# Linear attention on one core: the sum over a head's partitions for rows 0 to 511, made by four transfers inside SBUF and two adds on VectorE instead of one matrix product

## The chip, the core and the metric

The kernel runs on one core of a Trainium2 chip. The core has five engines that work side by side, each through its own list of instructions in order: TensorE (PE in the profile, with its weight loads listed as PEld), VectorE (DVE), ScalarE (ACT), GpSimd (POOL) and SyncE (SP), which here issues the transfers (DMA). Engines wait for each other through semaphores. SBUF is the on-chip memory of 128 partitions; PSUM, of eight banks of 128 x 512 f32, takes the results of matrix products.

The metric is the device time of one execution in microseconds (us), the median of several runs.

## What is computed

The reference, cut to what matters, with B = 1, S = 2048 rows, D = 640, H = 32 heads of Dh = 20:

```python
qkv = (x @ wqkv).reshape(B, S, 3, H, Dh)          # then split into q, k, v by heads
phi = lambda t: where(t > 0, t + 1, exp(t)) + 1e-6
pq, pk = phi(q), phi(k)
kv  = einsum("bhsd,bhse->bhde", pk, v)            # 20 x 20 per head
z   = einsum("bhsd->bhd", pk)                     # sum of pk over all rows
num = einsum("bhqd,bhde->bhqe", pq, kv)
den = einsum("bhqd,bhd->bhq", pq, z) + 1e-6       # one number per row and head
o   = num / den
out = o.reshape(B, S, D) @ wo
```

The change is about `den`: for every row and head the sum of 20 products of `pq` and `z`.

## The kernel before

**Layout.** The columns of q are reordered so that `pq` lies in SBUF as five chunks c = 0..4 of 128 partitions by 2048 rows of the sequence. A head's 20 columns are then 4 neighbouring partitions in each of the 5 chunks: head h has partitions 4h to 4h+3. The sequence is worked on in four blocks s = 0..3 of 512 rows.

**Stages.** First comes k: `k_half` (L292) for 16 row tiles, with `k_phi` making `pk` from it. Then `p_step` (L319) accumulates x^T pk over the 16 row tiles in five PSUM banks, first for the left half of the columns (h = 0) and then for the right half (h = 1); in the code one call of `p_step(h, st)` is one row tile, five products of 320 columns. Between these steps, at places written out by hand in the loops at the end of the kernel, stand *q tiles*: `next_q` calls `q_tile` (L345), five products of 512 columns into one bank, then an exponential on ACT (L353), then a min (L357) and a multiply-and-add (L360) on DVE, which leave one chunk of one block of `pq`. There are 20 q tiles, block by block.

After the right half, `p_out` copies the five banks to `pt` (ACT L331 for chunks 0, 2, 4; DVE L334 for chunks 1 and 3), `kv_group` (L423) multiplies that with the v weights, `kv_mask` (L440) keeps the diagonal blocks, and `w2_group` (L447, L451) multiplies them with wo; `w2_rows` (L459) brings each result into its place by a DMA on SP (`w2p`). At the end `out_tile` (L487) multiplies `pq` with `w2p`, 16 row tiles, and writes the output (DMA L497).

**The denominator.** `z_steps` adds up `pk` over row tiles on DVE (L366) and ends in `zs` (L387). `z_finish` (L397) sums `zs` over the partitions with five narrow products and copies the result to `zc` (L401): a factor for every partition and chunk. For each block s, `wsum(s, c)` makes the sum over the chunks of `pq` times `zc`: c = 0 on ACT (L408), c = 1 to 4 on DVE (L412), the last one into `ub`, 128 x 512 bf16. What is then missing is the sum over the four partitions of a head. `den(s, b)` makes it with one matrix product (L465) by a 0/1 matrix `hm`, which also leaves the result on all four partitions. `den_act` takes the logarithm (L470) and the exponential of its negative (L472) on ACT, which gives 1/den in `rd`, and `normalize` (L479) multiplies `pq` by it on DVE. `inverse(s)` is `den` and `den_act` together.

**What sets the order.** No scheduler: `P.add` appends an instruction to its engine's list in the order of the program text and works out the semaphore waits from what each instruction reads and writes. Deferred pieces stand in the list `todo`: `work("w0")` appends the five `wsum` of block 0, `"n0"` the five `normalize`, digits after the block select chunks; `pop(n)` and the argument of `next_q(n)` take them out, n pieces after a q tile. Small results (q tiles, `z_finish`, `den`) take PSUM banks from a rotation, `take()`, of banks 5, 6, 7, later 4 too.

Before the change, in the loop over `p_step(1, st)`: the last two z steps after st = 0 and 1; q tiles after st = 1, 4, 7, 10, 12; `z_finish` after st = 5, followed by three pieces of `wsum` for block 0; two more pieces each after the q tiles of st = 7 and 10; `inverse(0)` after st = 11. After `p_out(1)` three more pieces are taken and then the q tile with the state groups.

Of the kernel before, what the change touches and what calls it, by code (L numbers as in the profile page):

```python
# [6 lines left out]
ACTF = mybir.ActivationFunctionType  # L7
ALU = mybir.AluOpType
BF16 = mybir.dt.bfloat16
F32 = mybir.dt.float32  # L10
# [72 lines left out]
def bass_standalone__linear_attn_block__prompt_kernel(nc, x, wqkv, wo, out):  # L83
# [9 lines left out]
    BK = 512  # L93

    with contextlib.ExitStack() as ctx:
        es = ctx.enter_context

        def sb(name, cols, dt=BF16):
            return es(nc.sbuf_tensor(name, [128, cols], dt))
# [21 lines left out]
        ub = [sb(f"ub{j}", BK) for j in range(2)]  # L121
        bm = sb("bm", GW)
        ones = sb("ones", 8)
        eps = sb("eps", 8, F32)
        ident = sb("ident", 128)
        lb = [sb(f"lb{j}", BK, F32) for j in range(2)]
        rd = [sb(f"rd{j}", 2 * BK) for j in range(2)]
        DUO = range(9)
        osb = [sb(f"osb{j}", D) for j in range(4)]
        ps = es(nc.psum_tensor("ps", [128, 8 * BK], F32))  # L130

        P = Plan(nc, es)

        def bank(b, n=BK, off=0, parts=128):
            return ps[0:parts, BK * b + off:BK * b + off + n]
# [179 lines left out]
        def p_step(h, st, ds=range(NC_)):  # L315

            def mm(e):
                for d in ds:
                    r = e.matmul(  # L319
                        bank(d, HALF), xn[:, st * D + 128 * d:st * D + 128 * d + 128],  # L320
                        pk[:, st * D + HALF * h:st * D + HALF * (h + 1)],
                        start=(st == 0), stop=(st == NT - 1))
                return r
            P.add("pe", mm, reads=xn_keys(st) + [("pk", st)],
                  writes=[("bank", d) for d in ds])
# [13 lines left out]
        def q_tile(sbk, c, b, between=None):  # L339
            i = nq[0] % 3  # L340
            nq[0] += 1

            def mm(e):
                for d in range(NC_):
                    r = e.matmul(  # L345
                        bank(b), wqp[:, d * D + 128 * c:d * D + 128 * c + 128],
                        xT[:, d * S + BK * sbk:d * S + BK * (sbk + 1)],
                        start=(d == 0), stop=(d == NC_ - 1))
                return r
            P.add("pe", mm, reads=[("wqp", d) for d in range(NC_)]  # L350
                  + xT_keys(BK * sbk, BK * (sbk + 1)), writes=[("bank", b)])
            t = eq[i]
            P.add("act", lambda e: e.activation(t[:, :], bank(b), ACTF.Exp),  # L353
                  reads=[("bank", b), "table"], writes=[("eq", i)])
            if between:
                between()
            P.add("dve", lambda e: e.tensor_scalar(  # L357
                t[:, :], t[:, :], 1.0, 1e-6, ALU.min, ALU.add),
                reads=[("eq", i)], writes=[("eq", i)])
            P.add("dve", lambda e: e.scalar_tensor_tensor(  # L360
                pq[:, c * S + BK * sbk:c * S + BK * (sbk + 1)], bank(b), 0.0, t[:, :],
                ALU.max, ALU.add),
                reads=[("bank", b), ("eq", i)], writes=[("pq", sbk, c)])
# [30 lines left out]
        def z_finish(b):  # L394
            def mm(e):
                for c in range(NC_):
                    r = e.matmul(bank(b, 1, off=c), zs[:, 128 * c:128 * c + 128],  # L397
                                 ones[:, 0:1], start=True, stop=True)
                return r
            P.add("pe", mm, reads=["zs", "ones"], writes=[("bank", b)])  # L400
            P.add("dve", lambda e: e.tensor_copy(zc[:, 0:NC_], bank(b, NC_)),  # L401
                  reads=[("bank", b)], writes=["zc"])
# [61 lines left out]
        def den(s, b):  # L464
            P.add("pe", lambda e: e.matmul(bank(b), hm[:, :], ub[s % 2][:, :], start=True, stop=True),  # L465
                  reads=["hm", ("ub", s % 2)], writes=[("bank", b)])

        def den_act(s, b):
            t = lb[s % 2]
            P.add("act", lambda e: e.activation(t[:, :], bank(b), ACTF.Ln, bias=eps[:, 0:1]),  # L470
                  reads=[("bank", b), "eps", "table"], writes=[("lb", s % 2)])
            P.add("act", lambda e: e.activation(  # L472
                rd[s // 2][:, BK * (s % 2):BK * (s % 2 + 1)], t[:, :], ACTF.Exp, scale=-1.0),
                reads=[("lb", s % 2)], writes=[("rd", s)])
# [40 lines left out]
        def out_tile(st, b, mid=None, late=None):  # L515
# [4 lines left out]
            if late:  # L520
                late()
            if st in DUO:
                j = st % 4
# [23 lines left out]
        for k in order.split():  # L547
            st = int(k[1])
# [17 lines left out]
        todo = []  # L566
        small = [5, 6, 7]

        def take():
            small.append(small.pop(0))  # L570
            return small[-1]

        def next_q(n=1, between=None):
            q_tile(*qs.pop(0), take(), between)
            for _ in range(n):
                if todo:
                    todo.pop(0)()

        def inverse(s):
            b = take()  # L580
            den(s, b)
            den_act(s, b)

        def work(*names):
            for w in names:
                kind, s, cs = w[0], int(w[1]), w[2:] or "01234"
                for c in cs:
                    todo.append(lambda s=s, c=int(c), kind=kind:
                                (wsum if kind == "w" else normalize)(s, c))

        def pop(n):
            for _ in range(n):
                todo.pop(0)()
# [15 lines left out]
        for st in range(NT - 2):  # L609
            p_step(1, st)  # L610
            if st in (0, 1):
                zst.pop(0)()
            if st == 5:
                z_finish(take())
                work("w0", "w1", "n0")
                pop(3)
            if st in (1, 4, 7, 10, 12):
                next_q({7: 2, 10: 2}.get(st, 0))
            if st == 11:
                inverse(0)  # L620
        assert not zst
        for d in range(NC_):
            p_step(1, NT - 2, (d,))
# [23 lines left out]
        next_q(1)  # L647
        inverse(1)
        work("w20", "n1", "w21234")
        for n in (1, 2, 2):  # L650
            next_q(n)
        work("w30123")
        assert not qs
        small[:] = [6, 7]
# [48 lines left out]
```

## Time and profile before

| | |
|---|---|
| time, median of 3 runs | 99.43 us (99.31 to 99.62) |
| the profiled execution: its time, its span | 99.73 us, 98.5 us |
| granted TensorE clock | 1.00 |
| q tiles, products (L345) | 100 products, 24.2 us busy |
| `p_step` products (L319) | 160 products, 24.0 us busy |
| `den` products (L465) | 4 products of 512 columns |
| weighted sums on DVE (L412) | 16 instructions, 12.0 us busy |
| normalize on DVE (L479) | 20 instructions, 7.4 us busy |
| transfers in use between 40 and 64 us of the span | almost none: 0 to 7 GB/s |

How to read the profile: the span is the time from the first to the last instruction; the rest of an execution's time lies around it. Matrix products are pipelined and their ends are modelled, so a product's length in the timeline overlaps the next one's start; the distance between starts tells what one costs. In the timeline the bracket at the end of a row tells how long the engine was idle before it and what ended that. The chain of waits goes back from the last instruction to what released each one.

### The profile page before, as it was taken

How to read it: one execution, taken by the hardware profiler on the slowest of the kernel's cores; microseconds unless marked ns; L12 is line 12 of the kernel's file. 1: busy time of each engine (PE TensorE's matmuls, PEld its weight loads, DVE VectorE, ACT ScalarE, POOL GpSimd, SP SyncE). 2: the span in 40 equal slices, each digit the busy share in tenths (PEclk: the TensorE clock that was granted, in tenths of full speed). 3: DMA queues.
4: the chain of work that ended last, by engine and by line, in shares of the span. 5: the costliest groups of instructions: out<-in, count | busy, mean ns of one | idle time of the engine just before them, and what ended most of it. 6: DMA issues, size and time to landing. Idle time of an engine off the chain costs nothing.

```text
span 98.5 us, 1673 instructions
## 1 busy us (share of the span) xinstructions
PE 95.5 (97%) x657; PEld 62.4 (63%) x657; DVE 74.0 (75%) x138; ACT 50.3 (51%) x83; POOL 3.5 (4%) x15
## 2 busy tenths in 40 slices
PE   6999999999999999999999999999999999999992
PEld 2567777777777656556666556755446776667771
DVE  0214987888989897999849769999979998809332
ACT  5005553455499202372052476289796749665321
POOL 6800000000000000000000000000000000000000
DMA  2988799979999930000000000005600233312534
GB/s 22 379 174 142 156 185 134 224 217 367 378 363 313 204 82 2 3 0 0 0 7 0 0 0 0 0 0 158 168 17 0 85 115 133 133 69 71 200 133 133
DMA packets 17236, 11.73 MB, mean 119 GB/s; under 512 B 9933, under 2 KB 17229, under 8 KB 17229
## 3 DMA queue, kind: packets, MB, share of 16 engines
q1 hardware_dynamic: 16653, 11.10, 43.3%
q10 hardware_dynamic: 576, 0.53, 1.5%
q8 instruction: 5, 0.08, 0.4%
q14 instruction: 2, 0.02, 0.1%
HBM read 5.90 MB, written 2.62 MB: 87 GB/s over the span
## 4 chain that ended last, share of the span: by engine, by line
PE 94%; DMA 3%; DVE 0%; issue 0%
PE ps L292 23%; PE ps L487 22%; PE ps L319 22%; PE ps L345 22%; DMA xn<-in_x_dram 3%; PE ps L447 2%; PE ps L423 1%; PE ps L198 1%; PE ps L465 1%; DVE osb L512 0%; PE ps L397 0%
## 5 line engine op out<-in xcount | busy, mean ns | idle before, releaser
L345 PE MATMUL ps<-xT,wqp 128*128 128x512 bf16 x100 | 24.2, 379 | 0.0
L319 PE MATMUL ps<-pk,xn 128*128 128x320 bf16 x160 | 24.0, 299 | 0.0
L292 PE MATMUL ps<-wk,xT 128*128 128x320 bf16 x160 | 22.9, 304 | 0.0
L487 PE MATMUL ps<-w2p,pq 128*128 128x320 bf16 (+3 forms) x170 | 22.3, 291 | 0.0
L353 ACT ACTIVATE eq<-ps 128x512 bf16<-128x512 f32 x20 | 11.9, 597 | 19.1 <-PE ps L345 19.0
L319 PEld LDWEIGHTS ps<-pk,xn 128*128 128x128 bf16 x160 | 15.6, 98 | 7.5
L487 PEld LDWEIGHTS ps<-w2p,pq 128*128 128x128 bf16 x170 | 15.9, 98 | 6.4 <-DVE pq L479 0.2
L292 PEld LDWEIGHTS ps<-wk,xT 128*128 128x128 bf16 x160 | 15.9, 100 | 6.4 <-ACT xT L210 0.2
L305 ACT ACTIVATE ek<-ps 128x640 bf16<-128x640 f32 x16 | 11.2, 704 | 11.7 <-PE ps L292 11.1
L345 PEld LDWEIGHTS ps<-xT,wqp 128*128 128x128 bf16 x100 | 9.7, 98 | 9.2
L360 DVE SCALAR_TENSOR_TENSOR pq<-ps,eq 128x512 bf16<-128x512 f32 x20 | 13.8, 692 | 0.7
L310 DVE SCALAR_TENSOR_TENSOR pk<-ps,ek 128x640 bf16<-128x640 f32 x16 | 13.2, 825 | 0.6
L412 DVE SCALAR_TENSOR_TENSOR ua<-pq,zc,ua 128x512 f32<-128x512 bf16 x12 | 9.0, 748 | 1.1 <-ACT ua L408 0.9
L307 DVE TENSOR_SCALAR ek<-ek 128x640 bf16<-128x640 bf16 x16 | 5.2, 325 | 5.9 <-ACT ek L305 5.9
L479 DVE TENSOR_TENSOR pq<-pq,rd 128x512 bf16<-128x512 bf16 x20 | 7.4, 418 | 2.8 <-ACT rd L472 2.8
L357 DVE TENSOR_SCALAR eq<-eq 128x512 bf16<-128x512 bf16 x20 | 5.8, 288 | 4.1 <-ACT eq L353 3.9
L524 ACT CAST osb<-ps 128x640 bf16<-128x640 f32 x9 | 6.2, 688 | 3.6 <-PE ps L487 3.4
L512 DVE CAST osb<-ps 128x320 bf16<-128x320 f32 (+2 forms) x8 | 3.5, 435 | 3.3 <-PE ps L487 3.1
L366 DVE TENSOR_TENSOR za<-pk 128x1280 f32<-128x1280 bf16 x4 | 5.8, 1484 | 0.0
L509 ACT CAST osb<-ps 128x320 bf16<-128x320 f32 (+1 forms) x8 | 3.1, 404 | 4.7 <-PE ps L487 4.5
L366 DVE TENSOR_TENSOR za<-za 128x1280 f32<-128x1280 f32 x3 | 4.4, 1482 | 0.0
L270 ACT COPY wqp<-wqn 128x640 bf16<-128x640 bf16 x5 | 4.3, 932 | 0.0
(41 smaller groups left out, 43.8 us busy)
## 6 DMA issues: line engine op xcount, KB each, us to landing
out_dram<-osb SPq DMA_DIRECT2D x15, 160.0 KB, 1.8
xn<-in_x_dram SPq DMA_DIRECT2D x2, 800.0 KB, 10.9
wqn<-in_wqkv_dram SPq DMA_DIRECT2D x1, 800.0 KB, 7.1
wv<-in_wqkv_dram SPq DMA_DIRECT2D x1, 800.0 KB, 14.5
wog<-in_wo_dram SPq DMA_DIRECT2D x1, 750.0 KB, 12.8
w2p<-w2g SPq DMA_DIRECT2D x5, 150.0 KB
xn<-in_x_dram SPq DMA_DIRECT2D x1, 640.0 KB, 8.3
wk<-in_wqkv_dram SPq DMA_DIRECT2D x3, 160.0 KB, 3.7
```

What stands on the lines that cost most here:

```text
L292: r = e.matmul(bank(b + h, HALF), xT[:, c * S + 128 * st:c * S + 128 * st + 128], wk[:, c * D + HALF * h:c * D + HALF * (h + 1)], start=(c ...
L305: P.add("act", lambda e: e.activation(fold(t[:, :]), two_banks(b), ACTF.Exp), reads=banks + ["table"], writes=[("ek", st % 3)])
L310: P.add("dve", lambda e: e.scalar_tensor_tensor(fold(pk[:, st * D:(st + 1) * D]), two_banks(b), 0.0, fold(t[:, :]), ALU.max, ALU.add), rea ...
L319: r = e.matmul(bank(d, HALF), xn[:, st * D + 128 * d:st * D + 128 * d + 128], pk[:, st * D + HALF * h:st * D + HALF * (h + 1)], start=(st ...
L345: r = e.matmul(bank(b), wqp[:, d * D + 128 * c:d * D + 128 * c + 128], xT[:, d * S + BK * sbk:d * S + BK * (sbk + 1)], start=(d == 0), sto ...
L353: P.add("act", lambda e: e.activation(t[:, :], bank(b), ACTF.Exp), reads=[("bank", b), "table"], writes=[("eq", i)])
L360: P.add("dve", lambda e: e.scalar_tensor_tensor(pq[:, c * S + BK * sbk:c * S + BK * (sbk + 1)], bank(b), 0.0, t[:, :], ALU.max, ALU.add), ...
L366: P.add("dve", lambda e: e.tensor_tensor(d_ap, a, b, ALU.add), reads=ra + rb, writes=[dst])
L412: P.add("dve", lambda e: e.scalar_tensor_tensor(dst[:, :], v, z, a[:, :], ALU.mult, ALU.add), reads=[("pq", s, c), "zc", key], writes=[dkey])
L479: P.add("dve", lambda e: e.tensor_tensor(v, v, rd[i][:, BK * o:BK * (o + 1)], ALU.mult), reads=[("rd", sbk), ("pq", sbk, c)], writes=[("pq ...
L487: r = e.matmul(bank(b, hi - lo), pq[:, c * S + 128 * st:c * S + 128 * st + 128], w2p[:, c * D + lo:c * D + hi], start=(c == 0), stop=(c == ...
L524: P.add("act", lambda e: e.copy(fold(osb[j][:, :]), two_banks(b)), reads=[("bank", b), ("bank", b + 1)], writes=[("osb", j, c) for c in ra ...
```

## The change

For block 0 alone the sum over a head's partitions is made without TensorE. Right after the last `wsum` of block 0 has written `ub0`, SP issues four transfers (`spread`). Transfer k reads the 32 partitions k, k+4, k+8, ... of `ub0` (512 bf16, 1 KB each) and writes each of them to four neighbouring partitions of column block k of the new tile `pb` (128 x 2048 bf16). Afterwards the four column blocks of `pb` hold, on every partition, the four members of that partition's head. DVE adds the first two blocks to the last two (1024 columns, bf16 in, f32 out) and then the two halves of the result (512 columns, f32): `group_sum`, into `sm`. `den_act` reads `sm` instead of a PSUM bank.

The order by hand changes with it: `z_finish` and the first three weighted sums move from after `p_step(1, 5)` to after `p_step(1, 4)`, ahead of the q tile there; the pieces taken after the q tiles of st = 4, 7 and 10 become 2, 3 and 1; `inverse(0)` after st = 11 goes. In `todo` stand, in this order: the five sums of block 0, the four transfers (with the last of these sums), sums 0, 1 and 2 of block 1, the two adds, sums 3 and 4 of block 1, logarithm and exponential for block 0, the normalize of block 0. So on DVE the two adds come after the q tile of st = 10 and ahead of the q tile of st = 12, and logarithm and exponential on ACT come after the copies of `p_out(1)`. Blocks 1, 2 and 3 keep `inverse`.

```diff
+        pb = sb("pb", 4 * BK)
+        sm = sb("sm", 2 * BK, F32)
...
+        def spread(s):
+            for k in range(4):
+                P.add("sp", lambda e, k=k: e.dma_start(
+                    pb[:, BK * k:BK * (k + 1)],
+                    ub[s % 2][k:128:4, :].unsqueeze(1).broadcast_to([32, 4, BK])),
+                    reads=[("ub", s % 2)], writes=[("pb", k)], dma=True)
+
+        def group_sum(s, eng):
+            P.add(eng, lambda e: e.tensor_tensor(
+                sm[:, :], pb[:, 0:2 * BK], pb[:, 2 * BK:], ALU.add),
+                reads=[("pb", k) for k in range(4)], writes=["sm"])
+            P.add(eng, lambda e: e.tensor_tensor(
+                sm[:, 0:BK], sm[:, 0:BK], sm[:, BK:], ALU.add), reads=["sm"], writes=["sm"])
+
         def den_act(s, b):
             t = lb[s % 2]
-            P.add("act", lambda e: e.activation(t[:, :], bank(b), ACTF.Ln, bias=eps[:, 0:1]),
-                  reads=[("bank", b), "eps", "table"], writes=[("lb", s % 2)])
+            src, key = (sm[:, 0:BK], "sm") if b is None else (bank(b), ("bank", b))
+            P.add("act", lambda e: e.activation(t[:, :], src, ACTF.Ln, bias=eps[:, 0:1]),
+                  reads=[key, "eps", "table"], writes=[("lb", s % 2)])
...
         def work(*names):
             for w in names:
+                if w[0] == "d":
+                    last = todo.pop()
+                    todo.append(lambda last=last, s=int(w[1]): (last(), spread(s)))
+                    continue
+                if w[0] == "a":
+                    todo.append(lambda s=int(w[1]): den_act(s, None))
+                    continue
+                if w[0] == "g":
+                    todo.append(lambda s=int(w[1]): group_sum(s, "dve"))
+                    continue
...
-            if st == 5:
+            if st == 4:
                 z_finish(take())
-                work("w0", "w1", "n0")
+                work("w0", "d0", "w1012", "g0", "w134", "a0", "n0")
                 pop(3)
             if st in (1, 4, 7, 10, 12):
-                next_q({7: 2, 10: 2}.get(st, 0))
-            if st == 11:
-                inverse(0)
+                next_q({4: 2, 7: 3, 10: 1}.get(st, 0))
```

## The prediction

> **What bounds the kernel now.** I read the page first, for the engine that is busy throughout, then the chain of waits in order of time, to see whether that engine ever pauses. In the chain each row is start, length, what.
>
> ```profile
> span 98.5 us, 1673 instructions
> PE 95.5 (97%) x657; PEld 62.4 (63%) x657; DVE 74.0 (75%) x138; ACT 50.3 (51%) x83; POOL 3.5 (4%) x15
> ...
> 46.03 2.04 PE ps L319 x15
> 48.07 1.08 PE ps L345 x5
> 49.15 0.68 PE ps L319 x5
> 49.83 0.10 PE ps L397 x5
> 49.93 1.38 PE ps L319 x10
> 51.31 1.08 PE ps L345 x5
> ...
> 56.19 0.22 PE ps L465
> ...
> 60.20 1.08 PE ps L345 x5
> 61.28 1.43 PE ps L423 x30
> ```
>
> PE is the bound, and each piece starts where the one before it ends: 15 products of `p_step` always take 2.04 us (0.136 each), a q tile 1.08. No row of this stretch has a pause, so the change can win only what it takes out of PE's list, and everything that makes PE pause is lost in full. The product that goes, `den(0)` (L465), is worth 0.22 us.
>
> Second view: the timeline of the same stretch, start and length first, where DVE's and ACT's slack can be read. I need it to replay the new order.
>
> ```profile
> 46.71 1.33 DVE L387 TENSOR_TENSOR zs<-za 128x640 bf16<-128x640 f32 x1
> 47.91 1.24 PE L345 MATMUL ps<-xT,wqp 128*128 128x512 bf16 x5
> 48.28 0.69 DVE L360 SCALAR_TENSOR_TENSOR pq<-ps,eq 128x512 bf16<-128x512 f32 x1
> 49.19 0.60 ACT L353 ACTIVATE eq<-ps 128x512 bf16<-128x512 f32 x1 [2.52 <-PE ps L345]
> 49.53 0.31 PEld L397 LDWEIGHTS ps<-ones,zs 128*128 128x128 bf16 x5
> 49.66 0.27 PE L397 MATMUL ps<-ones,zs 128*128 128x1 bf16 x5
> 49.79 1.52 PE L319 MATMUL ps<-pk,xn 128*128 128x320 bf16 x10
> 49.81 0.29 DVE L357 TENSOR_SCALAR eq<-eq 128x512 bf16<-128x512 bf16 x1 [0.84 <-ACT eq L353]
> 50.14 0.69 DVE L360 SCALAR_TENSOR_TENSOR pq<-ps,eq 128x512 bf16<-128x512 f32 x1
> 50.75 0.15 DVE L401 COPY zc<-ps 128x5 f32<-128x5 f32 x1
> 50.94 0.72 ACT L408 ACTIVATE ua<-pq,zc 128x512 f32<-128x512 bf16 x1 [1.16 <-DVE zc L401]
> 51.78 1.54 DVE L412 SCALAR_TENSOR_TENSOR ua<-pq,zc,ua 128x512 f32<-128x512 bf16 x2 [0.88 <-ACT ua L408]
> 53.23 0.28 DVE L357 TENSOR_SCALAR eq<-eq 128x512 bf16<-128x512 bf16 x1
> 54.94 0.75 DVE L412 SCALAR_TENSOR_TENSOR ub<-pq,zc,ua 128x512 bf16<-128x512 bf16 x1
> 56.65 0.68 ACT L470 ACTIVATE lb<-ps,eps 128x512 f32<-128x512 f32 x1
> 57.36 0.63 ACT L472 ACTIVATE rd<-lb 128x512 bf16<-128x512 f32 x1
> 58.83 0.29 DVE L357 TENSOR_SCALAR eq<-eq 128x512 bf16<-128x512 bf16 x1 [0.98 <-ACT eq L353]
> 59.15 1.51 ACT L331 CAST pt<-ps 128x320 bf16<-128x320 f32 x3 [0.35 <-PE ps L319]
> 59.15 0.69 DVE L360 SCALAR_TENSOR_TENSOR pq<-ps,eq 128x512 bf16<-128x512 f32 x1
> 59.76 0.88 DVE L334 CAST pt<-ps 128x320 bf16<-128x320 f32 x2
> 60.03 1.24 PE L345 MATMUL ps<-xT,wqp 128*128 128x512 bf16 x5
> 61.11 1.60 PE L423 MATMUL ps<-pt,wv 128*128 128x120 bf16 x30
> 63.65 0.28 DVE L357 TENSOR_SCALAR eq<-eq 128x512 bf16<-128x512 bf16 x1
> ```
>
> DVE has three pauses here (0.84, 0.88, 0.98 us), so it is not the bound. But the two casts of `pt` (L334) end at 60.64, and the state products (L423), which need them, start on PE at 61.11: DVE may be about 0.3 us later there (a hand-off of 0.04, as from `zc`'s end at 50.90 to ACT's start at 50.94, and 0.13 from weight load to product, 49.53 to 49.66) before PE stops.
>
> **Part 1: one matrix product goes.** Minus 0.22 us (the chain's L465 row). Its bank is not taken, so the banks of all later q tiles shift by one place in the rotation of small banks; a q tile still finds a bank last used three or more tiles earlier, and I cost that at nothing; the cover is those tiles' PE time, over 1 us each.
>
> **Part 2: `z_finish` moves one step forward, ahead of a q tile.** Its products need `zs`, which DVE ends at 46.71+1.33 = 48.04, in an order nothing changes up to there. PE now has the q tile at 47.91; in the new order `z_finish`'s weight load waits until 48.04+0.04 = 48.08 and the first product starts at 48.21 (0.13 later). That is a new PE pause of 0.30 us. The products' own cost is only moved: five take 0.13 from start to the next start (49.66 to 49.79). The q tile starts at 48.34.
>
> From there PE's list is plain addition: q tile 1.08, three steps 2.04, q tile at 51.46; 1.08 and 2.04, q tile at 54.58; 1.08 and 1.36 (two steps, without `den`), q tile at 57.02; 1.08 and 2.04, q tile at 60.14 against 60.03 before; the state products at 61.22 if nothing stops them. So without the transfers PE stands 0.11 behind (0.30 less 0.22, and rounding).
>
> **Part 3: the weighted sums start earlier.** `zc` follows the multiply at 48.28+0.61 = 48.89 (0.61 is 50.14 to 50.75), ends at 49.04, ACT's first factor runs to 49.80, and DVE starts at 49.92 (0.12 later, as from 51.66 to 51.78). Two sums end at 51.46; then come the q tile's min and multiply and two more sums, 2.46 us from 53.23 to 55.69 in the row, which start about 0.09 before the end: 51.37 to 53.83. `ub0` is ready at 53.83 instead of 55.69.
>
> **Part 4: four transfers inside SBUF.** No transfer of this form is in the trace. These rows are the nearest (issue time on SP as min/median/max ns, then time to landing):
>
> ```profile
> L459 SPq DMA_DIRECT2D w2p<-w2g x6: 698/772/940, 65.0 to 69.6; - x6
> L497 SPq DMA_DIRECT2D out_dram<-osb x16: 332/332/385, 76.4 to 96.5; - x16
> ...
> DMA to landing us min/median/max: 1.6/1.8/4.1
> ...
> SPq L459 <- ACT w2g L451: 37.7, 4, 36.2
> ```
>
> SP waits for `ub0` and then issues the four one after the other. SP has been waiting 36.2 us in this stretch, and the next thing queued is the `w2p` copy at 65.04, so nothing there is held up. An issue costs between 0.33 (`out`: 128 rows on both sides) and 0.77, the first 0.94 (`w2p`: SBUF to SBUF, unlike partition shapes). The new one resembles `w2p` (SBUF to SBUF, 32 x 4 rows against 128) but keeps 128 rows of 1 KB, like `out`; I take 0.65, nearer `w2p`. From the end of an issue to landing, `out` (160 KB) takes 1.8-0.33 = 1.47; I use it for 128 KB. With 0.03 for SP to start, 0.04 between issues and 0.04 for the hand-off, starting from 53.81:
> - at 0.33: last issue ends 55.28, DVE may start at 56.79;
> - at 0.65: last issue ends 56.56, DVE may start at 58.07;
> - at 0.94 and three of 0.77: 57.21, 58.72.
>
> The Trainium skill, page "DMA: Bandwidth & Descriptors", section "Anatomy of one DMA", gives 2.0 us plus bytes/436e3 for a transfer, fitted on the GpSimd path: 2.3 us for 128 KB. The trace's own 160 KB store is below that rule (1.8 against 2.4). By this estimate from the page the last landing, from an issue at 55.91, is 58.21 in place of 58.03, and the forecast would be 100.39; I stay with the row.
>
> **Part 5: two adds on DVE, behind the transfers.** Their rows:
>
> ```profile
> L366 DVE TENSOR_TENSOR za<-pk 128x1280 f32<-128x1280 bf16 x4 | 5.8, 1484 | 0.0
> L412 DVE SCALAR_TENSOR_TENSOR ua<-pq,zc,ua 128x512 f32<-128x512 bf16 x12 | 9.0, 748 | 1.1 <-ACT ua L408 0.9
> ```
>
> In proportion to 1484 ns for 1280, the first add (1024) takes 1.19 and the second (512) 0.59; along the line between 748 at 512 and 1484 at 1280 they take 1.24 and 0.75. I take 1.21 and 0.67, with 0.04 between them: 1.92 (bounds 1.82 to 2.03).
>
> The Trainium skill, page "VectorE: DVE Perf Modes", section on the TRN2 errata, gives (N+151)/0.96 ns for an fp32 add of two tensors. For 1280 that is 1491, and the trace agrees (1484). By this estimate from the page the pair takes 1.96 with the gap, and the forecast would be 0.04 longer.
>
> When is DVE free for them? After `ub0` it does a q tile and two sums of the next block (ending about 56.2), then the q tile of 54.58: product 1.24, hand-off 0.04, exponential 0.60, 0.02, so its min starts at 56.48, the multiply at 56.81, and the adds could start at 57.42. From there: adds to 59.34, min at 59.26 (DVE overlaps ends by 0.08, as 59.84 and 59.76 show), multiply 59.58, casts 60.19 to 61.07, PE at 61.24, against 61.22: 0.02 lost. So there is no slack left: every tenth by which the landing is later than 57.42 becomes a tenth of PE pause. Behind the waiting add stand, in DVE's order, that min and multiply, the casts of `pt`, two sums and the masks; PE waits for the casts. At 58.07 the pause is 0.65+0.02 = 0.67.
>
> ACT's logarithm and exponential (0.68, 0.63) now stand behind its casts, which end at 60.66+0.11 = 60.77, so they end near 62.1 and the exponential of the next q tile near 62.7; DVE asks for that at 63.65 or later. Free, with about 1 us of cover; without that cover it would be the overshoot. After the state products the masks wait for PE again, so DVE's delay isn't handed on a second time, and nothing later on PE has a pause that could absorb it.
>
> **Sum.** -0.22 + 0.30 (0.03 rounding) + 0.67 = +0.78 us. The profiled execution took 99.73 (span 98.5 and 1.23 around it), 0.30 above the median of 99.43; 99.73 would become 100.51, so on the median: **100.21 us**.
>
> **Rivals.**
> 1. *Landed in time.* Issues at `out`'s 0.33 to about 0.48: the last landing is before 57.42 and only 0.11+0.02 is lost: 99.56, no difference that shows. For it: 128 even rows of 1 KB, an idle SP, no other traffic. Against: the one SBUF-to-SBUF row costs 0.77. This is the case on the other side; it decides at an issue of 0.48 (53.84+4x0.48+0.12+1.47+0.04 = 57.39).
> 2. *Full price of `w2p`.* DVE starts at 58.72, the pause is 1.32, sum +1.43: 100.86. For it: that row's form and its slow first issue of 0.94. Against: its last copy, with a third of the rows, still cost 0.70, so the price seems to be one of shape, and this shape is simpler.
> 3. *PE doesn't feel the wait for `zs`,* and the transfers land in time: only -0.22+0.02 remains, 99.23. For it: 0.30 is a difference of starts across engines. Against: DVE's end at 48.04 is plainly behind PE's 47.91.
>
> **How the numbers follow.** The forecast case (issue 0.5 to 0.72, times 99.7 to 100.6) has 0.50, rival 1 0.25, rival 2 and anything beyond it 0.19, rival 3 0.06. A measurement of this kernel can tell about 0.3% (0.30 us) from no change; faster by more would need gains beyond the 0.22 that the removed product holds, so only noise and an unseen effect are left: 0.05. Within 0.3%: rival 1, rival 3 and the forecast's lower edge, less those, 0.27. Slower: 0.68. The range goes from rival 1 less a little (99.5) to rival 2 plus a little (101.0).
>
> **What would show it.** PE: a pause of about 0.3 ahead of `z_finish` near 48, no hm product near 56, and a pause ahead of the state products near 61, ended by DVE's casts; the last is the term to look at. SP: four issues from about 53.8, 0.65 each. DVE: the first add idle before it, ended by a transfer, starting near 58.1; adds of 1.2 and 0.67. Rival 1 shows the add starting right behind a multiply near 57.4 with no idle time; rival 2 shows issues of 0.77. I am wrong in kind if PE pauses somewhere after 64, if the adds take well beyond 2.0, or if PE's total shrinks although it waits for `zs`.

## The result, and the profile after

The changed kernel takes 100.56 us (median of 6 runs, 100.19 to 101.05) against 99.37 for the kernel before (99.01 to 99.76): ratio 1.0112, 95% interval 1.0079 to 1.0145. That is 1.1 us slower (0.8 to 1.4); the forecast was 0.78 slower. The profiled execution took 100.60. All times here and below are of executions at a granted TensorE clock of 1.00; three of the six of run e7 ran at 0.98 and are not counted.

First the page of the changed kernel: the span, the engines, and the shares of the chain that ended last.

```profile
span 99.3 us, 1672 instructions
PE 94.7 (95%) x650; PEld 61.5 (62%) x656; DVE 75.6 (76%) x140; ACT 50.1 (50%) x83; POOL 3.5 (4%) x15
...
PE 68%; DVE 17%; DMA 7%; SPq 2%; ACT 2%; issue 1%; DVEq 0%
```

Before, PE held 94% of that chain. Now it runs for long stretches through DVE, SP and a transfer: PE has come to wait for them. Of the 7% for DMA the transfer into `pb` is 2.09 us; 4.43 us are a load of weights at the start of the chain. (The line numbers are 2 to 17 higher than before: L399 is `z_finish`, L425 the state products, L336 the casts of `pt`, L472 the transfers, L478 and L481 the adds.) The timeline of the changed kernel shows where:

```profile
45.55 2.20 PE L321 MATMUL ps<-pk,xn 128*128 128x320 bf16 x15
46.39 1.32 DVE L389 TENSOR_TENSOR zs<-za 128x640 bf16<-128x640 f32 x1
47.77 0.19 PEld L399 LDWEIGHTS ps<-ones,zs 128*128 128x128 bf16 x5 [0.35 <-DVE zs L389]
47.91 1.24 PE L347 MATMUL ps<-xT,wqp 128*128 128x512 bf16 x5
48.56 0.15 DVE L403 COPY zc<-ps 128x5 f32<-128x5 f32 x1
48.74 0.72 ACT L410 ACTIVATE ua<-pq,zc 128x512 f32<-128x512 bf16 x1 [2.40 <-DVE zc L403]
49.37 0.58 ACT L355 ACTIVATE eq<-ps 128x512 bf16<-128x512 f32 x1
50.00 1.54 DVE L414 SCALAR_TENSOR_TENSOR ua<-pq,zc,ua 128x512 f32<-128x512 bf16 x2 [1.29 <-ACT eq L355]
53.16 0.75 DVE L414 SCALAR_TENSOR_TENSOR ub<-pq,zc,ua 128x512 bf16<-128x512 bf16 x1
53.94 2.58 SPq L472 DMA_DIRECT2D pb<-ub  x4
56.53 0.69 DVE L362 SCALAR_TENSOR_TENSOR pq<-ps,eq 128x512 bf16<-128x512 f32 x1
58.20 1.22 DVE L478 TENSOR_TENSOR sm<-pb 128x1024 f32<-128x1024 bf16 x1 [0.99 <-DMA pb<-ub]
59.46 0.69 DVE L481 TENSOR_TENSOR sm<-sm 128x512 f32<-128x512 f32 x1
59.56 0.88 PEld L347 LDWEIGHTS ps<-xT,wqp 128*128 128x128 bf16 x5
61.00 0.88 DVE L336 CAST pt<-ps 128x320 bf16<-128x320 f32 x2
61.93 1.61 PE L425 MATMUL ps<-pt,wv 128*128 128x120 bf16 x30 [1.00 <-DVE pt L336]
```

Two pauses of PE are new. Ahead of `z_finish`: the 15 products of the step start at 45.55 and take 2.04, so PE was free at 47.59; the q tile starts at 47.91, 0.32 later, of which `z_finish` itself is 0.13. The pause is 0.19. Ahead of the state products: the q tile there starts at 59.56+0.13 = 59.69 and takes 1.08, so PE was free at 60.77; it starts at 61.93. The pause is 1.16. With the removed product the sum is -0.22+0.19+1.16 = +1.13, the measured difference. An independent check: from the q tile at 47.91 to the end of the last product were 48.60 us before (to 96.51) and are 49.44 now (to 97.35 in the chain below); 0.84 more, and 1.16-0.22-0.13 (`z_finish` now lies ahead of that tile) is 0.81. The two profiled executions differ by only 0.87 (100.60 and 99.73), because up to `zs`, in an order that the change leaves alone, the one profiled after was 0.33 ahead, and the 0.32 ahead of that tile used this up. Behind the pause nothing is lost: from the first state product to the end of the last product PE took 35.40 us before (61.11 to 96.51) and 35.42 now (61.93 to 97.35).

Now the last of the four transfers and what follows it, in the chain of waits of the changed kernel in order of time (start, length, what):

```profile
55.92 2.09 DMA pb<-ub
58.01 0.03 issue
58.04 0.02 DVEq L79
58.06 0.05 issue
58.11 0.05 DVEq L79
58.16 0.04 issue
58.20 1.24 DVE sm L478
...
97.35 0.02 issue
```

The last issue starts at 55.92, the transfer has landed at 58.01, and DVE then still passes several semaphore waits one after the other (L79) until 58.20. DVE had been idle since the multiply of 56.53, for 0.99 us by the bracket.

### The profile page after: what moved, and what is told of

Its sections match the earlier page's. It is cut to its first block, busy times and chain, and to the rows that moved or that the text cites. A ratio compares the mean times of both kernels' runs of the same rounds, so it can differ in the third digit from the quotient of the medians.

```text
span 99.3 us, 1672 instructions
## 1 busy us (share of the span) xinstructions
PE 94.7 (95%) x650; PEld 61.5 (62%) x656; DVE 75.6 (76%) x140; ACT 50.1 (50%) x83; POOL 3.5 (4%) x15
## 4 chain that ended last, share of the span: by engine, by line
PE 68%; DVE 17%; DMA 7%; SPq 2%; ACT 2%; issue 1%; DVEq 0%
PE ps L504 22%; PE ps L294 21%; PE ps L347 14%; PE ps L321 8%; DMA wk<-in_wqkv_dram 4%; DVE za L368 4%; DVE pq L362 3%; DVE ua L414 2%; DMA pb<-ub 2%; ACT eq L355 2%; SPq L472 2%; PE ps L449 2%; PE ps L425 2%; DVE eq L359 1%; DVE zs L389 1%; DVE sm L478 1%
## 5 line engine op out<-in xcount | busy, mean ns | idle before, releaser
L347 PE MATMUL ps<-xT,wqp 128*128 128x512 bf16 x95 | 23.1, 379 | 0.3
L294 PE MATMUL ps<-wk,xT 128*128 128x320 bf16 x160 | 22.4, 299 | 0.3 <-DMA wk<-in_wqkv_dram 0.3
L294 PEld LDWEIGHTS ps<-wk,xT 128*128 128x128 bf16 x160 | 15.4, 98 | 6.8 <-DMA wk<-in_wqkv_dram 0.6
```

Source lines behind the costliest of these rows:

```text
L294: r = e.matmul(bank(b + h, HALF), xT[:, c * S + 128 * st:c * S + 128 * st + 128], wk[:, c * D + HALF * h:c * D + HALF * (h + 1)], start=(c ...
L347: r = e.matmul(bank(b), wqp[:, d * D + 128 * c:d * D + 128 * c + 128], xT[:, d * S + BK * sbk:d * S + BK * (sbk + 1)], start=(d == 0), sto ...
```

## The experiments

Edits are shown against the changed kernel, unless the text says otherwise. All times are compared with the kernel of before on the same chip; its medians were 99.32 to 99.52 us in the three groups. "Pause" is PE's pause ahead of the state products, worked out as above: start of the q tile before them plus 1.08, up to their start.

| run | pause, us | time, us | ratio to before (95% interval) |
|---|---|---|---|
| the change | 1.16 | 100.56 | 1.0112 (1.0079 to 1.0145) |
| e1 adds late | 0 | 99.45 | 0.9992 (0.9967 to 1.0018) |
| e2 adds late, z after q tile | 0 | 99.49 | 0.9998 (0.9970 to 1.0025) |
| e3 early data | 0.08 | 99.66 | 1.0018 (0.9990 to 1.0046) |
| e4 one add | 0.36 | 99.95 | 1.0048 (1.0021 to 1.0074) |
| e5 idle transfers | 0 | 99.46 | 1.0009 (0.9984 to 1.0035) |
| e6 z forward only | 0 | 99.86 | 1.0040 (1.0014 to 1.0065) |
| e7 two queues | 2.14 | 101.34 | 1.0187 (1.0128 to 1.0247) |
| e8 first factor on DVE | 0.30 | 99.55 | 1.0024 (0.9999 to 1.0049) |
| e9 two queues, later | 0.22 | 99.61 | 1.0008 (0.9982 to 1.0033) |
| e10 short copy | 1.07 | 100.28 | 1.0090 (1.0062 to 1.0118) |
| e11 e2 and e8 together | 0 | 99.21 | 0.9964 (0.9938 to 0.9990) |

**e1: the adds behind the casts.** The theory says that the place of the adds costs, not the adds.

```diff
-                work("w0", "d0", "w1012", "g0", "w134", "a0", "n0")
+                work("w0", "d0", "w10123", "g0", "a0", "w14", "n0")
...
         p_out(1)
-        pop(3)
+        pop(1)
...
-        next_q(0, between=state_groups)
+        next_q(1, between=state_groups)
```

> The changed kernel, but the two adds stand on DVE behind the casts of pt, one sum of the second block (its last) goes behind the next q tiles, and logarithm and exponential stand behind the next q tile's exponential on ACT. Theory (the loss is PE's pause ahead of the state products, because the casts stand behind adds that wait for the transfers): that pause of about 1.2 us is gone, the pause ahead of z_finish (0.2 to 0.3) stays, and the time is that of before within 0.2 us (-0.22 + 0.2). Rival (the 1.9 us of adds or the transfers cost time wherever they stand): still 0.8 to 1.2 us slower than before.

99.45, no difference from before. The timeline of this run:

```profile
59.38 0.88 DVE L336 CAST pt<-ps 128x320 bf16<-128x320 f32 x2
59.65 1.24 PE L347 MATMUL ps<-xT,wqp 128*128 128x512 bf16 x5
60.17 1.22 DVE L478 TENSOR_TENSOR sm<-pb 128x1024 f32<-128x1024 bf16 x1
60.73 1.59 PE L425 MATMUL ps<-pt,wv 128*128 128x120 bf16 x30
61.42 0.69 DVE L481 TENSOR_TENSOR sm<-sm 128x512 f32<-128x512 f32 x1
62.03 0.94 DVE L442 TENSOR_TENSOR kvt<-ps,bm 120x480 bf16<-120x480 f32 x3
```

The casts end at 60.26, the state products start 60.73 = 59.65+1.08: no pause. The same two adds of the same length now stand behind the casts, where the kernel of before has three weighted sums of block 1. They, the transfers and the logarithm cost nothing there; the whole 1.1 us was their place in DVE's order.

**e2: in addition `z_finish` behind the q tile.** The edit is shown against e1.

```diff
-            if st == 4:
-                z_finish(take())
-                work("w0", "d0", "w10123", "g0", "a0", "w14", "n0")
-                pop(3)
             if st in (1, 4, 7, 10, 12):
-                next_q({4: 2, 7: 3, 10: 1}.get(st, 0))
+                next_q({7: 3, 10: 1}.get(st, 0))
+            if st == 4:
+                z_finish(take())
+                work("w0", "d0", "w10123", "g0", "a0", "w14", "n0")
+                pop(5)
```

> As the run with the late adds, and z_finish stands behind the q tile after the fifth step instead of ahead of it. Theory: neither pause is left, only the removed product counts, 0.2 us faster than before (0.1 to 0.3). Rival (the adds or the transfers cost time wherever they stand): 0.6 to 1.0 us slower than before. If the pause at z_finish was not a cost, the time equals that of the run with the late adds.

99.49: the expected 0.2 us did not show, and the time is that of e1, which by the expectation would mean that the pause at `z_finish` was no cost. The time can't decide that here. By the trace both pauses are gone, but a smaller one came in further on. Two rows of the timeline of this run:

```profile
63.86 0.68 ACT L453 CAST w2g<-ps 120x640 bf16<-120x640 f32 x1
64.60 0.46 PEld L449 LDWEIGHTS ps<-wog,kvt 120*120 120x120 bf16 x4 [0.40 <-ACT w2g L453]
```

Relative to PE's q tile the adds end 0.3 us later than in e1 (2.75 against 2.46 behind its start), and with them ACT's logarithm and the cast of `w2g` behind it, for which PE's next products wait: in the chain these four take 0.66 instead of 0.55. What remains, 0.1 us, is below what the interval can tell. What the pause at `z_finish` costs alone, e6 shows.

**e3: data that is ready early.** Adds, casts and order stay as in the change; the transfers carry something that has long been ready, so that rows 0 to 511 are divided by another number.

```diff
-                    ub[s % 2][k:128:4, :].unsqueeze(1).broadcast_to([32, 4, BK])),
-                    reads=[("ub", s % 2)], writes=[("pb", k)], dma=True)
+                    pk[k:128:4, 0:BK].unsqueeze(1).broadcast_to([32, 4, BK])),
+                    reads=[("pk", 0)], writes=[("pb", k)], dma=True)
```

> The changed kernel, but the four transfers read 512 columns of pk, which are ready long before, instead of ub0, so that rows 0 to 511 are divided by another number; adds, casts and order stay. Theory: the first add starts right behind the multiply ahead of it, 1.0 us earlier, PE's pause ahead of the state products shrinks from about 1.2 to 0.1 to 0.2 us, and the time is 0.1 to 0.3 us above before. Rival (DVE's extra 1.9 us and not the wait for the transfers): still about 1.1 us slower than before.

99.66, pause 0.08. The timeline of this run:

```profile
56.83 0.69 DVE L362 SCALAR_TENSOR_TENSOR pq<-ps,eq 128x512 bf16<-128x512 f32 x1
57.44 1.22 DVE L478 TENSOR_TENSOR sm<-pb 128x1024 f32<-128x1024 bf16 x1
60.00 1.24 PE L347 MATMUL ps<-xT,wqp 128*128 128x512 bf16 x5
61.16 1.60 PE L425 MATMUL ps<-pt,wv 128*128 128x120 bf16 x30
```

The add starts 0.61 behind the start of the multiply, without idle time. With the adds at the change's own place, it was the wait for the transfers that made 1.08 of the 1.16. The remaining 0.08 shows that DVE had no slack left to give, as the prediction had worked out (0.02).

**e4: one add.** The second add is left out, so that rows 0 to 511 are divided by half of the sum.

```diff
-            P.add(eng, lambda e: e.tensor_tensor(
-                sm[:, 0:BK], sm[:, 0:BK], sm[:, BK:], ALU.add), reads=["sm"], writes=["sm"])
```

> The changed kernel without the second add, so that rows 0 to 511 are divided by half of the sum. Theory (no slack at the casts, every DVE delay becomes a PE pause one to one): the casts end 0.7 us earlier, the pause ahead of the state products goes from about 1.2 to 0.5 us, and the time is 0.7 us below the changed kernel, 0.4 to 0.6 above before. Rival (PE waits there for something else than DVE's casts): the time of the changed kernel, 1.1 above before.

99.95. The pause goes from 1.16 to 0.36, by 0.80. The add is 0.69 with 0.04 ahead of it; the first add also started 0.07 earlier relative to PE's q tile, nearly all of it a shorter hand-off (0.13 from the last landing at 57.78 to the add, 0.19 in the change). DVE's delay reaches PE one to one.

**e5: the transfers alone,** in the kernel of before, with nobody reading `pb`.

```diff
...
             if st == 11:
+                spread(0)
                 inverse(0)
```

> The kernel of before with the four transfers added behind ub0 and nobody reading what they bring. Theory (only the wait for them costs): the time of before within 0.2 us, every product, sum and cast as long as before. Rival (the transfers slow the engines through SBUF or SP): 0.3 to 1 us slower, with longer DVE or ACT instructions between 55 and 60 us.

99.46, within the interval of no difference; the sums beside the transfers keep 0.74 to 0.75 us each. Landing four times 128 KB in SBUF slows nothing that can be seen.

**e6: only `z_finish` forward,** in the kernel of before, `den(0)` kept.

```diff
-            if st == 5:
+            if st == 4:
                 z_finish(take())
...
-                next_q({7: 2, 10: 2}.get(st, 0))
+                next_q({4: 2, 7: 2}.get(st, 0))
```

> The kernel of before with z_finish and the weighted sums one step earlier, as the change has it, but the matrix product den(0) kept at its place and no transfers. Theory: PE pauses 0.2 to 0.3 us ahead of z_finish and nowhere else, 0.2 to 0.3 us slower than before. Rival (the earlier start is free): the time of before. Rival (the order of the sums is what costs): about 1 us slower.

99.86: 0.4 us slower (0.1 to 0.6). The expectation of 0.2 to 0.3 lies in the interval, and the trace has the same wait of the weight load: a pause of 0.19, and none behind it (48.48 us from the q tile to the last product's end; before, without `z_finish`, 48.47). From the timeline of this run:

```profile
48.37 0.19 PEld L397 LDWEIGHTS ps<-ones,zs 128*128 128x128 bf16 x5 [0.35 <-DVE zs L387]
```

So the move of `z_finish` costs about what the removed product brings; the change could hardly have won even with transfers that cost no time, as e1 shows too.

**e7 and e9: two queues.** e7 lets ACT issue transfers 2 and 3, at the same place of the program.

```diff
-                P.add("sp", lambda e, k=k: e.dma_start(
+                P.add(("sp", "act")[k // 2], lambda e, k=k: e.dma_start(
```

> The changed kernel with transfers 2 and 3 issued by ACT instead of SP. Theory (four issues of 0.6 us one after the other make the last landing late): the last issue starts 1.2 to 1.3 us earlier, the first add starts 1.0 us earlier, right behind the multiply, the pause ahead of the state products shrinks to 0.1 to 0.3 us, and the time is 0.1 to 0.4 us above before. Rival (the transfers themselves or their landing are slow, not the issues): the first add starts no earlier and the time is that of the changed kernel, 1.1 above before.

101.34, about 2 us slower than before (1.3 to 2.5), and it does not answer the question. ACT's list had the two issues ahead of an exponential, and ACT waited there for `ub0`. The timeline of e7:

```profile
53.57 1.26 ACTq L472 DMA_DIRECT2D pb<-ub  x2
54.88 0.60 ACT L355 ACTIVATE eq<-ps 128x512 bf16<-128x512 f32 x1 [5.29 <-PE ps L321]
55.51 0.29 DVE L359 TENSOR_SCALAR eq<-eq 128x512 bf16<-128x512 bf16 x1 [1.96 <-ACT eq L355]
```

ACT stood idle for 5.29 us; the trace names PE as what ended that, but ACT's issues at 53.57, right at the end of `ub0`, show what it waited for. DVE then stood idle 1.96 for the exponential. e9 puts the two issues behind ACT's next exponential and factor:

```diff
...
-                work("w0", "d0", "w1012", "g0", "w134", "a0", "n0")
+                work("w0", "d0", "w10", "e0", "w112", "g0", "w134", "a0", "n0")
```

Here `"e0"` appends transfers 2 and 3, on ACT, to the first factor of block 1, and `"d0"` issues 0 and 1 on SP.

> The changed kernel with transfers 2 and 3 issued by ACT, and this time behind ACT's exponential and first factor of the second block, so that ACT doesn't wait for ub0 ahead of them. Theory (four issues of 0.6 us one after the other make the last landing late): the first add starts about 1.0 us earlier relative to PE, without idle time ahead of it, the pause ahead of the state products shrinks from 1.2 to 0.1 to 0.3 us, and the time is 0.1 to 0.4 us above before. Rival (the landing and not the issue is slow): the time of the changed kernel, 1.1 above before.

99.61, pause 0.22. From the timeline of e9:

```profile
53.95 1.54 SPq L472 DMA_DIRECT2D pb<-ub  x2
53.95 1.25 ACTq L472 DMA_DIRECT2D pb<-ub  x2
56.53 0.69 DVE L362 SCALAR_TENSOR_TENSOR pq<-ps,eq 128x512 bf16<-128x512 f32 x1
57.27 1.22 DVE L478 TENSOR_TENSOR sm<-pb 128x1024 f32<-128x1024 bf16 x1
```

With `ub0` at the same moment the last transfer lands at 57.24 instead of 58.01 and the add starts at 57.27 instead of 58.20. So four issues in one queue were a large part of the late landing. Two issues less in the queue are 1.28 us (0.60 and 0.04 each), of which the last landing gained 0.77: SP's second issue now took 0.84 instead of 0.59, and its transfer landed 2.59 after its start instead of 2.12. The Trainium skill, page "DMA: Bandwidth & Descriptors", section "Issuing engines are not separate DMA queues", says that several issuing engines save only the time to initiate a transfer, usually small beside the transfer. The trace agrees on what is saved, but here it was not small: the four issues take 2.58 of the 4.07 us from the first issue (53.94) to the last landing (58.01), and 0.77 of these 4.07 were saved.

**e8: the first factor on DVE.** In the change DVE was idle 1.29 us between `zc` and the first sum.

```diff
+            if c == 0 and s == 0:
+                P.add("dve", lambda e: e.tensor_scalar(
+                    a[:, :], v, z, 0.0, ALU.mult, ALU.add),
+                    reads=[("pq", s, c), "zc"], writes=[key])
+                return
             if c == 0:
                 P.add("act", lambda e: e.activation(a[:, :], v, ACTF.Copy, scale=z),
```

> The changed kernel with the first weighted factor of block 0 made on DVE (0.3 to 0.6 us there) instead of on ACT, so that DVE does not wait for ACT between zc and the first sum. Theory (ub0 comes late because DVE waits 1.3 us there, 0.4 longer than the prediction had): ub0 and the landing come 0.6 to 0.9 us earlier, the pause ahead of the state products shrinks from about 1.2 to 0.3 to 0.6 us, and the time is 0.2 to 0.6 us above before. Rival (ub0's time doesn't decide): the time of the changed kernel.

99.55, pause 0.30. From the timeline of e8, where the first sum follows `zc`'s start (48.41) after 0.71 instead of 1.44:

```profile
48.59 0.48 DVE L410 TENSOR_SCALAR ua<-pq,zc 128x512 f32<-128x512 bf16 x1
49.12 1.54 DVE L419 SCALAR_TENSOR_TENSOR ua<-pq,zc,ua 128x512 f32<-128x512 bf16 x2
57.20 1.23 DVE L483 TENSOR_TENSOR sm<-pb 128x1024 f32<-128x1024 bf16 x1 [0.28 <-DMA pb<-ub]
```

The wait for the transfers falls from 0.99 to 0.28. When `ub0` is ready decides as well.

**e10: why the first sum is late.** A copy of 8 columns on ACT behind the factor, ahead of the exponential.

```diff
...
+                if s == 0:
+                    P.add("act", lambda e: e.copy(dum[:, :], eps[:, :]),
+                          reads=["eps"], writes=["dum"])
                 return
```

> The changed kernel with a short copy of 8 columns on ACT behind each first factor of block 0, ahead of the exponential. Question: why DVE's first weighted sum starts at the end of ACT's next exponential (0.54 us behind the factor's end) when one follows directly, and 0.12 behind it when none does. Theory 1 (a factor's signal comes out only with the instruction queued right behind it): the sum starts at the end of the short copy, about 0.2 to 0.3 us behind the factor, ub0 and the adds come 0.25 us earlier and the time is 0.2 us below the changed kernel. Theory 2 (DVE waits for the exponential itself): the sum starts later than now, by the copy's 0.2 us.

Neither theory came out. From the timeline of e10:

```profile
49.16 0.72 ACT L411 ACTIVATE ua<-pq,zc 128x512 f32<-128x512 bf16 x1 [2.39 <-DVE zc L404]
49.79 0.18 ACT L414 COPY dum<-eps 128x8 f32<-128x8 f32 x1
49.88 0.59 ACT L356 ACTIVATE eq<-ps 128x512 bf16<-128x512 f32 x1
50.44 1.54 DVE L418 SCALAR_TENSOR_TENSOR ua<-pq,zc,ua 128x512 f32<-128x512 bf16 x2 [1.31 <-ACT dum L414]
```

The sum starts 0.56 behind the factor's end (49.88), as in the change (0.54), not at the end of the short copy (49.97), and not 0.2 later. It starts even 0.03 ahead of the exponential's end, so it does not wait for that. The trace's record of the semaphores settles theory 1: ACT's signal for the factor came 0.01 behind its end (49.90), and DVE had passed its wait for it at 49.94, 0.50 before the sum started. The factor's signal isn't late; what lies between is not told by the trace. The time, 100.28, can't be told from the change's.

**e11: e2 and e8 together.** Nothing else is edited.

> The kernel with the late adds and z_finish behind the q tile, and with the first factor of block 0 made on DVE. Theory: no pause ahead of z_finish and none ahead of the state products, the adds end before ACT needs them, so only the removed product counts: 0.2 us faster than before (0.1 to 0.3). Rival (DVE's extra instructions cost elsewhere): the time of before or above.

99.21, faster than before by 0.4% (0.1 to 0.6). The state products start right behind their q tile, and DVE's earlier sums bring the adds forward, so that ACT's casts of `w2g` are in time again. From the timeline of e11:

```profile
59.44 1.24 PE L347 MATMUL ps<-xT,wqp 128*128 128x512 bf16 x5
60.52 1.59 PE L430 MATMUL ps<-pt,wv 128*128 128x120 bf16 x30
```

From the q tile of 47.53 to the last product's end (95.92) this run has 48.39 us, against 48.60 before: 0.21 less, the one product that was removed. This is what was expected.

## Why the prediction was right, and what was off in its sizes

**What bounds the kernel, and what can be won.** Right. PE's list sets the end; e11, without pauses, wins just the product's 0.22.

**Part 1, the product.** Right: it was worth its 0.22, and the shifted banks cost nothing that shows (35.42 us against 35.40 from the state products on).

**Part 2, `z_finish`.** Right in kind, too large: 0.30 predicted, 0.19 by the starts in the trace. The weight load waited for `zs` as forecast (0.06 behind its end), but the products follow it faster than the 0.13 I had taken from the run of before. e6 shows the cost alone.

**Part 3, the weighted sums.** This is the term that was mis-sized. In the profile after, everything up to `zs` lies 0.33 earlier (`zs` ends at 47.71, not 48.04), so `ub0` should have been ready at 53.83-0.33 = 53.50; it was ready at 53.91, 0.41 later. I took 0.12 from the end of ACT's factor to DVE's first sum, as in the kernel of before; it was 0.54. Why it was 0.54 stays open (last section). e8, which takes ACT out of this step, moves `ub0` and the adds forward and removes most of the pause; it shows that `ub0`'s time decides, not where the 0.42 comes from.

**Part 4, the transfers.** Right. The issues took 0.59 to 0.66 each where I had 0.65, and landing came 1.49 behind the end of the last issue, where I had 1.47. That the issues one after the other make the landing late is shown by e9; that nothing else of the transfers costs time, by e5. One hand-off was too small: 0.19 instead of 0.04 between landing and add, with DVE's passes through its semaphore waits between them; in e4, e8 and e10 it was 0.07 to 0.13. By the rule of the Trainium skill's page "DMA: Bandwidth & Descriptors", section "Anatomy of one DMA", issue to landing takes, as an estimate, 2.3 us; the trace has 2.09, so the rule, fitted on the GpSimd path, is too high here.

**Part 5, the adds.** Right: 1.22 and 0.69, against 1.21 and 0.67. The Trainium skill's formula in "VectorE: DVE Perf Modes", section on the TRN2 errata, gives, as an estimate, 1224 and 691 ns; the trace (1224 and 692) agrees, closer than with either of my bounds. Logarithm and exponential on ACT were free as forecast: the next q tile's exponential ended at 62.09, and DVE asked for it at 64.10. That DVE had no slack behind 57.42 is shown by e3, that every delay there becomes a pause of PE by e4, and that the place of the adds decides by e1.

**The sum.** The pause ahead of the state products was 1.16 instead of 0.67, 0.49 more. On DVE, 0.41 came from `ub0`, 0.15 from the hand-off and 0.06 from landing and adds, less 0.14 from the issues: 0.48. Two more terms cancel. The state products followed the casts' end (61.88) after 0.05, where I had 0.17; and PE was free 0.12 earlier than forecast, because the pause at `z_finish` was shorter and DVE, which follows its own list from `zs` on, gained nothing by that. So what PE saved at `z_finish` it waited for here. With 0.49 more here, 0.11 less at `z_finish` and without the 0.03 of rounding, +0.78 became +1.13. The mechanism was the one forecast; the size was 0.35 too small, and the time, 100.56, lies at the upper end of the forecast case (99.7 to 100.6).

**The rivals.** "Landed in time" is what e3 and e9 make by hand, and their times (99.66, 99.61) agree with its 99.56. The full price of `w2p` for an issue was not paid (0.59 to 0.66, not 0.77), though the time came near that rival's 100.86 by another way: the time alone could not have told the two apart, the issues in the trace do. PE did feel the wait for `zs`.

## What to carry to other kernels

When one engine sets the end without a pause, a piece of work taken off it is worth its own time only if no wait is put in front of that engine; here 0.22 us was bought with waits of 1.35. A wait for a late transfer belongs, in an engine's order, behind what the bound engine needs next: the same adds cost 1.1 us ahead of the casts and nothing behind them. Count the issues in one queue as part of a transfer's latency, and look what stands behind an issue that waits, above all on an engine that also computes (e7).

## What the runs showed of the hardware that was not expected

How soon DVE starts its first sum behind ACT's factor. In the kernel of before, e2 and e5 it takes 0.12 to 0.13 us from the factor's end (before: 51.66 to 51.78). In the change (49.46 to 50.00) and in the seven runs that keep its `z_finish` ahead of the q tile and its factor on ACT, it takes 0.53 to 0.56. In these eight, ACT goes on at once with its next instruction, in the other three it has nothing to do; but the place in the order differs too, so that ACT's next instruction is the cause is not shown. e6, which has no transfers, shows it as well, so it isn't they. The bracket names ACT's exponential as what ended DVE's idle time, but the record of the semaphores says otherwise: in the change ACT's signal for the factor came at 49.48 and DVE had passed its wait for it at 49.52, 0.48 before the sum started; in the kernel of before it passed at 51.72, 0.06 before. So the time lies between the passed wait and DVE's start. What fills it stays open; e8 avoids it.

A transfer of 128 KB inside SBUF, 32 partitions read four times each, costs its issuing engine 0.59 to 0.66 us on SP and 0.61 on ACT, about twice a store of 160 KB to memory (0.33), and lands 2.08 to 2.14 us behind the start of its issue. In e3, where the four were issued near 27 us, among the loads from memory, they landed after 9.4 to 10.4. When SP and ACT issued at once (e7, e9), SP's second issue took 0.83 and 0.84, and the landings came after 2.12 to 2.60.
